# Three zero fills of a decode-attention backward kernel: two row blocks each of about 112 rows become one block of 208 to 223 rows

## The chip, the cores and the metric

The kernel runs on one core of a Trainium2 chip. The metric is the device time of one launch in microseconds (us), as the median of several runs.

## The reference, cut to what matters

The program computes a forward pass and all its gradients: attention of one query position over the last 4096 positions of a key and value cache, gated by a small two-layer network. What matters here is the size of two of the outputs, the gradients of the caches. Only the last W positions of 32768 take part, so the gradient of all the earlier ones is zero, and yet it has to be written.

```python
B, Hq, Hkv, Sk, Dh = 2, 32, 8, 32768, 128
W = min(4096, max(256, Sk // 4))              # 4096
k = jnp.repeat(k_cache[:, :, Sk - W:, :], rep, axis=1)
v = jnp.repeat(v_cache[:, :, Sk - W:, :], rep, axis=1)
scores = jnp.einsum("bhqd,bhkd->bhqk", q, k) * (Dh ** -0.5)
p = _softmax(scores, axis=-1)
o = jnp.einsum("bhqk,bhkd->bhqd", p, v)
...
s = attention(xn) @ wo
g = silu(relu(xn @ w1 + b1) ** 2 @ w2 + b2)
return x + s * g          # and its vjp with grad_out, for every input
```

Each cache gradient has 2 x 8 heads of 32768 rows of 256 bytes (128 bf16 values). Of every head 28672 rows (7168 KB) are zeros: 32 such blocks, 235 MB in all, of some 280 MB written.

## The kernel before, in words

**The zero fills.** There are 32 fills, numbered 0 to 31, one for each head of `out_2` (key gradient) and `out_3` (value gradient). They are copied by DMA from `zt`, an SBUF tile of 14336 zero bytes in each of 128 partitions. `zf` (L90) makes one DMA of a fill: `nent` entries (one row of the access pattern each) of `rows` consecutive cache rows, `rep` times over. The DMA casts while it copies. Up to 112 rows the zero bytes become bf16, two bytes out for one byte in. Above 112 rows the output is looked at as float32, four bytes out for one byte in, so that one entry can reach 224 rows, 57344 bytes:

```python
w = rows * DH
if w > ZG * DH:           # ZG = 112
    v = v.bitcast(F32)
    w //= 2
```

Fills 0 to 30 go out in order on POOL's (GpSimd's) DMA queue, L229 to L233. Those in `zlong` are one DMA of 128 entries of 224 rows. The eight in `zshort` are divided: a few small DMAs on a few entries, a main part of 128 entries, and a rest of single rows. In fills 2, 4, 6, 13 and 20 the main part is one DMA; in 8, 10 and 15 it is two, of 112 rows and of 96, 107 or 111 rows. POOL has eight DMA semaphores for these and waits with each issue for the DMA that is eight places ahead of it. The first fill waits for the load of `wo` (L235). Fill 31 goes out at the very end on SP's queue (`fin`, L640), in rows of 14336 bytes, after every other DMA that SP issues.

**The attention.** Four rounds, each for one batch entry and four key heads. Tiles `vnat` and `knat` hold the 4096 positions of a round's values and keys, in 128 partitions of 32768 bytes. Each has one buffer only, so a round goes so:

- `scores` (transposes at L383, matmuls at L390) over `vnat`, then over `knat`;
- the softmax and its gradient (L437 to L465);
- `outer_store` (its matmul is L417) for the values: the gradient is written over `vnat`, and stored on ACT's queue (L421); then SP loads the next round's values into the same tile (L210), as soon as that store has landed;
- the same for the keys: `contract` (its matmul is L406), `outer_store`, the store on ACT's queue, the next load on SP's queue.

So at the end of each round there is a chain: store, load into the same tile, and then the next round's `scores`.

**The end.** After the fourth round come the weights' gradients: `wq` is stored at L580 and `wo` at L586 (ACT's queue), `w2T` at L609, `dw` at L635 and fill 31 at L640 (SP's queue).

Of the kernel before, what the change touches and what calls it, by code (L numbers as in the profile page):

```python
# [16 lines left out]
def kernel(  # L17
# [72 lines left out]
    def zf(o, q, r0, nent, rows, rep=1):  # L90
# [18 lines left out]
        2: ((5, 8, 2), (120, 68, 3), (128, 32, 1), (16, 1, 1)),  # L109
        4: ((3, 1, 2), (2, 99, 6), (128, 214, 1), (86, 1, 1)),  # L110
        6: ((3, 1, 2), (3, 53, 2), (128, 221, 1), (60, 1, 1)),
        8: ((4, 82, 6), (128, 112, 1), (128, 96, 1), (80, 1, 1)),
        10: ((4, 69, 2), (128, 112, 1), (128, 107, 1), (88, 1, 1)),
        13: ((2, 20, 2), (3, 30, 2), (128, 221, 1), (124, 1, 1)),
        15: ((4, 1, 2), (128, 112, 1), (128, 111, 1), (120, 1, 1)),
        20: ((4, 25, 2), (128, 222, 1), (56, 1, 1)),
    }
    eps_t = const.tile([P, 1], F32, name="eps_t")
# [552 lines left out]
```

## Time and profile before

| | |
|---|---|
| median of 3 runs | 764.79 us (764.75 to 764.82) |
| profiled execution, its own time | 764.8 us |
| its span, first to last instruction | 763.0 us |
| bytes moved, mean rate | 326.73 MB, 428 GB/s |
| of these on POOL's queue (q0) | 227.55 MB in 6784 packets |
| on SP's queue (q1) / ACT's queue (q10) | 56.63 MB / 41.95 MB |
| busy: TensorE / VectorE / ScalarE | 52% / 36% / 28% |

A packet is the piece that a DMA engine moves at one go; the core has 16 DMA engines, and each queue has a share of the packets of every one of them. The profile gives for a stretch of time the number of packets of each queue, their bytes, and the time that they took as a share of the 16 engines. [...]

### The profile page before, as it was taken

To read this page: it belongs to the slowest core of one execution; us is meant where nothing else is said; L and a number is where in the kernel's file an instruction comes from. 1 tells how busy PE (TensorE), PEld (TensorE's weight loads), DVE (VectorE), ACT (ScalarE), POOL (GpSimd) and SP (SyncE) were. 2 spreads that over 40 slices of the span, in tenths; PEclk is the share of its full clock that TensorE was granted. 3 is DMA by queue.
4 is the path that set the end of the run, shared out by engine and by line. 5 is a ranking of instruction groups with operands and counts; after the bars stand their busy time and mean duration, and the time that the engine had idled before them with its cause. 6 is when DMAs were issued, how large, how long until landed. Compare 5 with 4: busy or idle time off the path is not lost.

```text
span 763.0 us, 9422 instructions
## 1 busy us (share of the span) xinstructions
PE 398.6 (52%) x4127; PEld 242.3 (32%) x4136; DVE 274.7 (36%) x481; ACT 216.7 (28%) x314; POOL 32.0 (4%) x63
## 2 busy tenths in 40 slices
PE   5866973853035748640187485002644784866900
PEld 4742552420023534210055341002433443323200
DVE  4334342823012455330054555001324451665600
ACT  3253323523001145430022455000114230721600
POOL 0200000000000100000000000000000000000000
PEclk9986896766558857665579577555767595855555
DMA  9999999999999999999999999999999999999998
GB/s 382 439 424 437 410 443 434 435 423 433 419 436 440 419 440 434 427 426 431 431 429 443 431 431 422 432 430 445 426 436 437 431 434 434 415 432 434 421 426 378
DMA packets 10973, 326.73 MB, mean 428 GB/s; under 512 B 2548, under 2 KB 2557, under 8 KB 2586
## 3 DMA queue, kind: packets, MB, share of 16 engines
q0 software_dynamic: 6784, 227.55, 70.4%
q1 hardware_dynamic: 2696, 56.63, 21.1%
q10 hardware_dynamic: 1452, 41.95, 15.2%
q8 instruction: 32, 0.52, 0.3%
q14 instruction: 9, 0.07, 0.0%
HBM read 45.62 MB, written 280.50 MB: 427 GB/s over the span
## 4 chain that ended last, share of the span: by engine, by line
PE 34%; DMA 33%; DVE 12%; ACT 10%; issue 7%; ACTq 0%; DVEq 0%; SPq 0%
DMA out_dram<-nat 16%; DMA nat<-in_A_k_cache_dram 10%; PE ov L417 7%; PE tp L383 6%; DMA nat<-in_A_v_cache_dram 5%; ACT tring L150 3%; ACT p_bf L451 2%; ACT nat L150 2%; DVE nat L152 2%; PE ps L406 2%; PE s_ps L390 2%; DVE ds_bf L464 2%; PE wps L584 2%; PE dops L331 1%; DVE tring L152 1%
## 5 line engine op out<-in xcount | busy, mean ns | idle before, releaser
L383 PE MATMUL tp<-pperm,nat 128*128 128x128 bf16 x1024 | 93.3, 244 | 178.0 <-DMA nat<-in_A_v_cache_dram 146.1
L152 DVE COPY tring<-tp 128x1024 bf16<-128x1024 bf16 (+1 forms) x98 | 66.3, 689 | 192.1 <-PE tp L383 188.7
L383 PEld LDWEIGHTS <-nat 128*128 128x128 bf16 x1024 | 69.4, 109 | 198.4 <-DMA nat<-in_A_v_cache_dram 148.1
L150 ACT CAST nat<-ov 128x512 bf16<-128x512 f32 x160 | 87.7, 590 | 78.5 <-PE ov L417 57.7
L150 ACT COPY tring<-tp 128x1024 bf16<-128x1024 bf16 (+1 forms) x34 | 34.4, 1011 | 247.6 <-PE tp L383 220.6
L152 DVE CAST nat<-ov 128x512 bf16<-128x512 f32 x96 | 65.7, 690 | 69.3 <-PE ov L417 66.9
L417 PE MATMUL ov<-bd,ds_bf 128*128 128x512 bf16 x124 | 50.0, 483 | 19.0 <-issue 12.9
L101 POOL DMA_DIRECT2D out_dram<-zt x54 | 30.4, 567 | 531.3 <-DMA out_dram<-zt 510.1
L417 PE MATMUL ov<-bd,p_bf 128*128 128x512 bf16 x123 | 46.7, 447 | 5.5 <-ACT nat L150 1.4
L406 PE MATMUL ps<-t,nat 128*128 128x16 bf16 x1024 | 28.8, 173 | 18.2 <-issue 11.4
L406 PEld LDWEIGHTS <-nat 128*128 128x128 bf16 x1024 | 28.7, 103 | 21.1 <-issue 16.0
L152 DVE CAST wq<-wps 128x512 bf16<-128x512 f32 x16 | 11.0, 690 | 54.4 <-PE wps L577 54.2
L390 PEld LDWEIGHTS <-zz 128*32 128x32 bf16 x512 | 17.6, 96 | 33.6 <-issue 23.5
L150 ACT CAST wq<-wps 128x512 bf16<-128x512 f32 x16 | 9.4, 586 | 63.6 <-PE wps L577 63.6
L390 PE MATMUL s_ps<-tring,zz 128*32 128x256 bf16 x256 | 20.0, 301 | 11.2 <-ACT tring L150 7.5
L398 PE MATMUL tp<-ident_bf,p_bf 128*128 128x128 bf16 x64 | 7.5, 310 | 34.9 <-ACT p_bf L451 34.9
L390 PE MATMUL dp_ps<-tring,zz 128*32 128x256 bf16 x256 | 20.0, 319 | 7.4 <-ACT tring L150 5.0
L451 ACT ACTIVATE p_bf<-e_sb,rl 32x512 bf16<-32x512 f32 x16 | 22.8, 1423 | 3.4 <-DVE rl L448 3.3
L417 PEld LDWEIGHTS <-ds_bf 128*128 128x128 bf16 x128 | 13.4, 111 | 27.4 <-issue 25.6
L464 DVE SCALAR_TENSOR_TENSOR ds_bf<-dp_ps,delta,p_bf 32x512 bf16<-32x512 f32 x16 | 21.6, 1352 | 0.2
L417 PEld LDWEIGHTS <-p_bf 128*128 128x128 bf16 x128 | 12.8, 109 | 19.7 <-issue 16.8
L398 PEld LDWEIGHTS <-p_bf 128*128 128x128 bf16 x64 | 6.5, 144 | 35.8 <-ACT p_bf L451 35.8
(198 smaller groups left out, 465.1 us busy)
## 6 DMA issues: line engine op xcount, KB each, us to landing
out_dram<-zt POOLq DMA_DIRECT2D x23, 7168.0 KB, 98.8
out_dram<-nat ACTq DMA_DIRECT2D x8, 4096.0 KB, 41.3
nat<-in_A_v_cache_dram SPq DMA_DIRECT2D x4, 4096.0 KB, 38.4
nat<-in_A_k_cache_dram SPq DMA_DIRECT2D x4, 4096.0 KB, 39.6
out_dram<-zt POOLq DMA_DIRECT2D x2, 7072.0 KB, 68.9
out_dram<-zt POOLq DMA_DIRECT2D x3, 3584.0 KB, 93.2
out_dram<-zt SPq DMA_DIRECT2D x1, 7168.0 KB, 35.0
out_dram<-zt POOLq DMA_DIRECT2D x1, 7104.0 KB, 120.6
```

The lines of the kernel that those rows point to most:

```text
L101: sw_fill.append(nc.gpsimd.dma_start(out=v, in_=zs))
L150: nc.scalar.copy(out=out_ap, in_=in_ap)
L152: nc.vector.tensor_copy(out=out_ap, in_=in_ap)
L331: nc.tensor.matmul(dops[0:B, :, :], lhsT=dsT_bf[:, dk, :], rhs=woT[:, :, dk, :], start=(dk == 0), stop=(dk == DK - 1))
L383: nc.tensor.transpose(tp[:, j, :], nat[:, g * CC + half * CH + j, :], pperm[:].rearrange("p b k -> p (b k)"))
L390: nc.tensor.matmul(out_ps[pr * RB:(pr + 1) * RB, half * CH * PB:(half + 1) * CH * PB], lhsT=zbuf[:, pr, o:o + RB], rhs=tT[:, :, pr, :], st ...
L398: nc.tensor.transpose(tp[:, cc, :], src[:, half * CH + cc].rearrange("r k b -> r (k b)"), ident_bf[:, :])
L406: nc.tensor.matmul(ps[:], lhsT=nat[:, g * CC + half * CH + cc, :], rhs=cols[half][:, cc, :, g, :], start=(half == 0 and g == 0 and cc == 0 ...
L417: nc.tensor.matmul(ov[:], lhsT=src[:, cc].rearrange("r k b -> r (k b)"), rhs=bd[:, gh * 4:(gh + 1) * 4, :], start=True, stop=True)
L451: nc.scalar.activation(out=p_bf[rb, :, :, pr], in_=e_sb[rb], func=ACT.Copy, scale=rl[rb, 0:1])
L464: nc.vector.scalar_tensor_tensor(out=ds_bf[rb, :, :, pr], in0=dp_c[rb], scalar=delta[rb, 0:1], in1=p_bf[rb, :, :, pr], op0=ALU.subtract, o ...
L584: nc.tensor.matmul(wps[:], lhsT=o_rows[:, j:N:NJ], rhs=ds_rows[:, :], start=True, stop=True)
```

## The change

The main part of fills 8, 10 and 15 becomes one DMA of 128 entries of 208, 219 or 223 rows (53248, 56064 and 57088 bytes an entry) and takes the float32 way of `zf`. The small parts ahead of it and the rest behind it stay as they are.

```diff
-        8: ((4, 82, 6), (128, 112, 1), (128, 96, 1), (80, 1, 1)),
-        10: ((4, 69, 2), (128, 112, 1), (128, 107, 1), (88, 1, 1)),
+        8: ((4, 82, 6), (128, 208, 1), (80, 1, 1)),
+        10: ((4, 69, 2), (128, 219, 1), (88, 1, 1)),
...
-        15: ((4, 1, 2), (128, 112, 1), (128, 111, 1), (120, 1, 1)),
+        15: ((4, 1, 2), (128, 223, 1), (120, 1, 1)),
```

## The prediction

> **What bounds the kernel now.** I read the page first, for how full the DMA engines are, then windows over single stages, then the timelines of SP and of TensorE for who waits where. The page's second part:
>
> ```profile
> DMA  9999999999999999999999999999999999999998
> GB/s 382 439 424 437 410 443 434 435 423 433 419 436 440 419 440 434 427 426 431 431 429 443 431 431 422 432 430 445 426 436 437 431 434 434 415 432 434 421 426 378
> ```
>
> The 16 DMA engines are full from the first slice to the last, while TensorE has half of its span. So the end is set by the bytes: 326.73 MB at 428 GB/s are 763 us. The fills (70% of the bytes) are filler that moves whenever nothing else does. The chain of compute costs time only where it leaves the DMA engines without work. That is the question for this change: it leaves the bytes written alone, but it alters **how long a load waits beside a fill**.
>
> The loads of the keys for rounds 2, 3 and 4, on SP's timeline, and what TensorE did about two of them, on its own timeline (in brackets the idle time ahead and what ended it):
>
> ```profile
> 217.44 0.54 SPq L210 DMA_DIRECT2D nat<-in_A_k_cache_dram  x1
> 375.28 0.54 SPq L210 DMA_DIRECT2D nat<-in_A_k_cache_dram  x1
> 516.33 0.54 SPq L210 DMA_DIRECT2D nat<-in_A_k_cache_dram  x1
> ```
>
> ```profile
> 250.74 1.89 PE L383 MATMUL tp<-pperm,nat 128*128 128x128 bf16 x16 [8.28 <-DMA nat<-in_A_k_cache_dram]
> 562.38 1.89 PE L383 MATMUL tp<-pperm,nat 128*128 128x128 bf16 x16 [12.40 <-DMA nat<-in_A_k_cache_dram]
> ```
>
> From issue to landing these three equal loads of 4096 KB took 33.3, 25.9 and 46.0 us (landed at 250.7, 401.2, 562.3). TensorE waited 8.3 us for the first and 12.4 us for the third. For the second it waited not at all, but without reserve: its timeline runs straight from the value transposes into the key transposes at about 401.4, 0.2 us after the landing. By the packet records, the first load ran beside fill 8, the second beside fill 15, both in halves of about 112 rows, and the third beside whole fills of 224 rows. (Fill 10's main part moved at about 257 to 280, when no load or store was under way, so its change costs nothing.)
>
> Why the third is slow can be read from the queues in two windows, 226:238 (first load, fill 8) and 530:548 (third load, whole fills):
>
> ```profile
> DMA packets 187, 5.21 MB, mean 435 GB/s; under 512 B 14, under 2 KB 14, under 8 KB 14
> ...
> q1 hardware_dynamic: 91, 2.92, 57.0%
> q0 software_dynamic: 95, 2.28, 44.8%
> ```
>
> ```profile
> DMA packets 192, 7.77 MB, mean 431 GB/s; under 512 B 15, under 2 KB 15, under 8 KB 15
> ...
> q0 software_dynamic: 95, 4.59, 59.3%
> q1 hardware_dynamic: 97, 3.18, 42.1%
> ```
>
> In both, fill packets and load packets go one for one (95 to 91, 95 to 97). The rate is the same, 435 and 431 GB/s, but the load's part of it is 2.92 of 5.21 MB against 3.18 of 7.77 MB.
>
> [...] here one row of 57344 bytes is one packet. [...] In the trace this is a packet of 4 bytes on each engine, and it is where the third load loses much. In the stretch 552.9:556 fourteen of them held 163% of the engines:
>
> ```profile
> q1 hardware_dynamic: 14, 0.00, 163.2%
> ```
>
> That is 1.632 x 16 x 3.1 / 14 = 5.8 us each, spent behind fill packets of over 2.1 us; 11 of that load's 16 took 6.4 us. Those of the first and second load took 0.03 us each, beside halves. [...]
>
> **The change part by part.**
>
> *Work of the DMA engines.* Per engine and fill, eight packets of 28 KB and eight of 24 to 28 KB become eight of 53 to 57 KB. In the packet records 28672 bytes take 1.079 us, 24576 take 0.928 and 57344 take 2.155. Two halves of fill 8 (2.007 us) against 53248 bytes at the long rows' rate (2.001 us): 0.006 us x 8 packets is 0.05 us. With three fills and three semaphore packets fewer, the gain is **0.2 us at most**. Half as many SBUF bytes are read, which buys nothing, since 28 KB and 56 KB rows already run at one rate. POOL issues 51 fill DMAs, not 54; at 0.57 us each that is 1.7 us of an engine with 32 us of work, hidden behind its waits. Its eight semaphores then reach further ahead in bytes, and since fills already wait 32 us or more from issue to landing, their queue is not empty either way.
>
> *Key load of round 2 (beside fill 8).* Now: a turn is 0.448 x 16 x 12 / 95 = 0.905 us for a fill packet and 0.570 x 192 / 91 = 1.20 for a load packet; eight turns (128 packets over 16 engines) are 16.9 us. After: from the other window 0.593 x 288 / 95 = 1.80 us for 48.3 KB, so 1.98 for 53248 bytes, and 1.25 for the load; eight turns are 25.9. The start, from issue to first packet, was 4.2, 6.7 and 10.3 us in the three loads; it is bounded by these, and I take 7. For the semaphore 0 to 10.6 us were seen, and I take the commonest beside long rows, 6.4. Sum 39.3, against 33.3 now: **+6.0 us**. It is not more, because the present landing is that of one straggling engine: its last packet began at 248.4, where seven eighths of all had begun by 237.7, since it was already in fill 9's long rows. Bounds: 0 (every engine just like the straggler) and +12.7 (like the third load, 46.0).
>
> *Key load of round 3 (beside fill 15).* No straggler here: 25.9 us. After: 7 + 8 x (2.12 + 1.25) + 6.4 = 40.4, so +14.5, less the 0.2 of reserve: **+14.3 us**. Bounds: 4.2 + 27.0 + 0 = 31.2, so +5, and 46.0, so +20.
>
> The loads and stores of round 4 already run beside long rows and stay as they are. Behind a late key load stands everything of the round: the key scores, the softmax, both stores on ACT's queue and the next two loads on SP's. So the sum carries to the last instruction: the compute is late by 6.0 + 14.3 = **20.3 us** (5 to 32.7).
>
> *What of it reaches the end.* Two more windows, after the issue of the `wo` store (712.5) and of the last DMA (727.1); the last two columns are the DMA share and GB/s:
>
> ```profile
> 712.50:727.10 14.60, 12.13 (x29) 3.29 (x27) 9.10 (x15) 8.44 (x15) 0.00 (x0) 0.50 0.99 421
> 727.10:763.00 35.90, 0.00 (x0) 0.00 (x0) 0.00 (x0) 0.00 (x0) 0.00 (x0) 0.50 0.93 400
> ```
>
> The last four DMAs (`wo` 4.19 MB, `w2T` and `dw` 1.84 each, fill 31 7.34) are 15.2 MB, and after 727.1 still 35.9 x 400 = 14.4 MB of them move. So of the 6.15 MB between 712.5 and 727.1 all but 0.8 are older: when `wo` is issued, the engines have 5.3 MB, 12.6 us at 421 GB/s, in hand. With the other queues slower the fills are faster, so this older work still ends at about 726. A `wo` store that comes later than that, less a start of some 1 us, finds idle engines. **The reserve is about 12 us** (10 to 14), and past it the end moves one for one: 20.3 - 12 = +8.3 us. With the 0.2 of gain this is +8 on the profiled execution's 764.8 us (span 763.0 and 1.8 around it), which is the median's 764.79 as well: **773 us**.
>
> **The rivals.** *The reserve swallows it* (not slower): the delay at `wo` stays under 12 us. The place is the gap between the older DMA work and the `wo` store, the price 20.3 us against 12, and it decides at 12. For it: the straggler, which may make round 2 cost nothing, and the semaphores, which are late beside long rows in some transfers only (the value load landing at 378.4 had nine of 16 on time); with both, 5 to 9 us. Then 764.6 us, the byte bound less 0.2. Against it: round 3's turns alone add 8.6 us, without any late semaphore. *Every wait at its worst*: 46 us for both loads and later stores that lose the help they now get from small packets (while a fill's single rows pass, each 256-byte packet costs a store one turn of some 0.03 us). Then 32.7 - 12 and more, 785 us. *Faster*: less for the engines to do is worth 0.2 us; beyond that only the uneven finish could give, and the last slice at 378 GB/s leaves about 2 us in it; 763 us at best. *That it doesn't do what it says*: rows of 57344 bytes already go as single packets, so rows of 53 to 57 KB will too.
>
> **How the numbers follow.** Two runs' medians can be told apart here from about 0.2%, 1.5 us, so slower begins at a delay of 13.5 us. Of my 5 to 32.7 us, most lies above: slower 0.72, of which 0.1 for the worst case; swallowed 0.22; faster 0.06. The range goes from the swallowed case, 764.2, to just short of the worst, 784.
>
> **What would show it.** Right: the key loads of rounds 2 and 3 take some 39 and 40 us, TensorE waits about 14 us for each, the last fill but one lands near 726 as now, and a gap in the DMA row stands ahead of the `wo` store, with all slices before it full. Wrong: the loads stay under 34 and 30 us, or the last instructions come 20 us later with no gap and no later end, or the rate in the middle falls under 425 GB/s.

## The result and the profile after

The changed kernel takes **786.6 us** (median of 6 runs, 782.59 to 799.47) against 764.88 us. It is slower, as forecast, but by 21.7 us and not by 8, and outside the range (764.2 to 784). The run at 799.47 us, more than 1.5% above the fastest of this kernel, is left out of the ratio of the two means, which is **1.0269** (95% interval 1.0246 to 1.0292). The profiled execution took 787.2 us with a span of 785.4, 22.4 us longer than before.

The page's second part, of the kernel after; compare the third number from the right of the GB/s row:

```profile
DMA  9999999999999999999999999999999999999099
GB/s 383 429 433 429 418 447 423 439 419 430 432 439 436 426 433 425 434 432 435 427 435 437 433 429 431 423 437 428 433 431 438 436 423 442 415 430 398 1 382 392
```

The same bytes (326.73 MB) move at the same rate (431 GB/s in the stretch 20:700 of both), except in one slice, in which nothing moves. In two windows, up to the `wo` store and from it on (columns as in the prediction: the last two are DMA share and GB/s):

```profile
726.50:748.00 21.50, 17.58 (x49) 8.08 (x50) 13.61 (x23) 7.67 (x14) 0.00 (x0) 0.50 0.00 1
748.00:785.40 37.40, 11.50 (x27) 3.09 (x25) 8.54 (x15) 8.13 (x14) 0.00 (x0) 0.50 0.96 407
```

The gap of 21.5 us is nearly the whole loss of 22.4. ACT issues the store at its end, first the line of the kernel before, then of the kernel after:

```profile
712.50 0.37 ACTq L586 DMA_DIRECT2D out_dram<-wo  x1
```

```profile
747.35 0.37 ACTq L586 DMA_DIRECT2D out_dram<-wo  x1
```

That is 34.9 us later than before; the store's first packet begins 0.9 us after its issue. The older DMA work was done at about 726.5, as forecast. The delay arises between two places in round 3, on SP's and TensorE's timelines. SP after, then TensorE before and after:

```profile
376.95 0.54 SPq L210 DMA_DIRECT2D nat<-in_A_k_cache_dram  x1
```

```profile
401.38 0.62 PE L383 MATMUL tp<-pperm,nat 128*128 128x128 bf16 x8
```

```profile
429.30 1.04 PE L383 MATMUL tp<-pperm,nat 128*128 128x128 bf16 x8 [21.09 <-DMA nat<-in_A_k_cache_dram]
```

The key load of round 3 is issued 1.7 us later than before and lands 28.0 us later, at 429.25 where it was 401.2: 52.3 us in place of 25.9. TensorE, which had not waited for it at all (the line of before has no wait), waits 21.1 us.

### The profile page after: what moved, and what is told of

Its sections match the earlier page's. It is cut to its first block, busy times and chain, and to the rows that moved or that the text cites. A ratio compares the mean times of both kernels' runs of the same rounds, so it can differ in the third digit from the quotient of the medians.

```text
span 785.4 us, 9428 instructions
## 1 busy us (share of the span) xinstructions
PE 396.8 (51%) x4136; PEld 240.0 (31%) x4136; DVE 274.9 (35%) x481; ACT 216.4 (28%) x314; POOL 30.3 (4%) x60
## 2 busy tenths in 40 slices
DMA packets 10541, 326.73 MB, mean 416 GB/s; under 512 B 2500, under 2 KB 2509, under 8 KB 2538
## 4 chain that ended last, share of the span: by engine, by line
PE 32%; DMA 31%; DVE 11%; ACT 9%; issue 7%; another core or an unknown queue 7%; SPq 0%; ACTq 0%; DVEq 0%
DMA out_dram<-nat 15%; DMA nat<-in_A_k_cache_dram 10%; PE tp L383 6%; PE ov L417 6%; DMA nat<-in_A_v_cache_dram 5%; ACT tring L150 3%; ACT p_bf L451 2%; PE s_ps L390 2%; ACT nat L150 2%; DVE ds_bf L464 2%; DVE nat L152 2%; PE wps L584 2%; PE ps L406 1%; PE wps L577 1%
## 5 line engine op out<-in xcount | busy, mean ns | idle before, releaser
L150 ACT COPY tring<-tp 128x1024 bf16<-128x1024 bf16 (+1 forms) x34 | 34.4, 1011 | 278.7 <-PE tp L383 253.8
L417 PE MATMUL ov<-bd,ds_bf 128*128 128x512 bf16 x128 | 50.5, 477 | 21.1 <-issue 15.9
L417 PE MATMUL ov<-bd,p_bf 128*128 128x512 bf16 x128 | 49.2, 457 | 4.0 <-DVE nat L152 1.4
L101 POOL DMA_DIRECT2D out_dram<-zt x51 | 28.7, 569 | 514.2 <-DMA out_dram<-zt 493.2
L406 PE MATMUL ps<-t,nat 128*128 128x16 bf16 x1024 | 28.9, 173 | 18.3 <-issue 11.4
L406 PEld LDWEIGHTS <-nat 128*128 128x128 bf16 x1024 | 28.8, 103 | 21.1 <-issue 16.0
L398 PE MATMUL tp<-ident_bf,p_bf 128*128 128x128 bf16 x64 | 7.6, 312 | 34.9 <-ACT p_bf L451 34.9
L464 DVE SCALAR_TENSOR_TENSOR ds_bf<-dp_ps,delta,p_bf 32x512 bf16<-32x512 f32 x16 | 21.7, 1359 | 0.2
L417 PEld LDWEIGHTS <-p_bf 128*128 128x128 bf16 x128 | 13.0, 110 | 19.6 <-issue 16.8
```

The lines of the kernel that those rows point to most:

```text
L101: sw_fill.append(nc.gpsimd.dma_start(out=v, in_=zs))
L150: nc.scalar.copy(out=out_ap, in_=in_ap)
L398: nc.tensor.transpose(tp[:, cc, :], src[:, half * CH + cc].rearrange("r k b -> r (k b)"), ident_bf[:, :])
L406: nc.tensor.matmul(ps[:], lhsT=nat[:, g * CC + half * CH + cc, :], rhs=cols[half][:, cc, :, g, :], start=(half == 0 and g == 0 and cc == 0 ...
L417: nc.tensor.matmul(ov[:], lhsT=src[:, cc].rearrange("r k b -> r (k b)"), rhs=bd[:, gh * 4:(gh + 1) * 4, :], start=True, stop=True)
L464: nc.vector.scalar_tensor_tensor(out=ds_bf[rb, :, :, pr], in0=dp_c[rb], scalar=delta[rb, 0:1], in1=p_bf[rb, :, :, pr], op0=ALU.subtract, o ...
```

## The experiments

The kernel before ran beside each of these, at 764.82 to 764.89 us; "wo" is the time at which the `wo` store is issued (712.5 before). Unless said otherwise, a time is the median.

### One fill at a time

`e1_only15`, `e2_only8` and `e3_only10` each take one line of the change:

```diff
-        15: ((4, 1, 2), (128, 112, 1), (128, 111, 1), (120, 1, 1)),
+        15: ((4, 1, 2), (128, 223, 1), (120, 1, 1)),       # e1; fills 8 and 10 likewise in e2, e3
```

Expected of fill 15 alone:

> Fill 15 alone in one block of 223 rows (fills 8 and 10 as before). Theory T: the loss is the key load of round 3, which meets long fill rows and a completion write queued behind them. Then nearly all of the loss is here: the key load of round 3 takes some 45 to 55 us (25.9 before), the wo store is issued some 30 to 36 us later, and the end is 18 to 24 us later, 782 to 788 us. Rival S (all three edits add up): about a third to a half, 770 to 778 us. Rival P (three DMAs fewer move POOL's eight places and the order in time): a third, about 772 us.

Measured: 786.2 us, ratio 1.0277 (1.0260 to 1.0294). Key load of round 3 53.8 us, wo at 746.25.

Expected of fill 8 alone:

> Fill 8 alone in one block of 208 rows. Theory T: the key load of round 2 lands within 3 us of before, because one engine was already in long rows there; the wo store is late by less than the reserve of 12 us; 764.6 to 765.5 us. My forecast's term: 6 us later at wo, and still no later end. Rival S: 770 to 778 us. Rival P: about 772 us.

Measured: 764.75 us, ratio 1.0002 (0.9993 to 1.0010). Key load of round 2 landed at 249.5 (250.7 before), wo at 712.85.

Expected of fill 10 alone:

> Fill 10 alone in one block of 219 rows. Theory T: nothing, its main part moves when no load or store is under way: 764.6 to 765.2 us. Rivals S and P: 770 us or more.

Measured: 764.92 us, ratio 1.0000 (0.9991 to 1.0009). Two of its 13 executions were long ones: the profiled one, 769.18 us with wo at 729.3, which comes in useful below, and one of 801.29 us without a profile.

So **fill 15 alone makes the loss**, and the edits do not add up.

### Number of DMAs, length of rows, or the cast

`e4_short51` has 51 fill DMAs like the changed kernel, but short rows:

```diff
+        8: ((4, 82, 6), (128, 104, 2), (80, 1, 1)),
+        10: ((4, 69, 2), (128, 109, 2), (108, 2, 1)),
+        15: ((4, 1, 2), (128, 111, 2), (124, 2, 1)),
```

> As few fill DMAs as in the changed kernel (51), but rows of 104 to 111: the main parts of fills 8, 10 and 15 are each one DMA of 128 entries, two rows blocks each (128,104,2), (128,109,2), (128,111,2), with the rest of fills 10 and 15 in entries of two rows. Theory T: the length of the rows decides, so this is as before: 764.5 to 766 us, key load of round 3 at 24 to 30 us. Rival P: as the changed kernel, 780 us or more.

Measured: 764.85 us, ratio 1.0000 (0.9991 to 1.0008); key load of round 3 26.9 us. The number of DMAs and POOL's semaphores have no part in it.

`e6_f32short` keeps the length of fill 15's two halves, and changes the cast alone:

```diff
-        if w > ZG * DH:
+        if w > ZG * DH or (o is out_2 and q == 15 and rows > 90):
```

> The kernel before, with fill 15's two halves (112 and 111 rows) written as float32 too: rows of 28 KB out of 7 KB of zeros. Same packets as before by length, but each is read from as few bytes a byte written as the long rows are. Theory L (the length of a packet written decides): as before, key load of round 3 at 24 to 30 us, 764.6 to 765.5 us. Rival C (the float32 cast decides, [...]): the load starts some 10 us late and its completion writes wait 5 us or more; key load at 38 us or more, and 770 us or more.

Measured: **784.26 us**, ratio 1.0251 (1.0223 to 1.0279). TensorE's timeline shows the landing of the changed kernel, to 0.1 us:

```profile
429.30 1.04 PE L383 MATMUL tp<-pperm,nat 128*128 128x128 bf16 x8 [27.57 <-DMA nat<-in_A_k_cache_dram]
```

So it is not the length of the row, as I had it, but **the float32 cast**, four bytes written for each byte read. The packet records show where it works first. The time from the issue of round 3's key load to its first packet is 6.7 us beside bf16 halves, 11.8 beside rows of 223 by the float32 cast, 12.0 beside halves by the float32 cast. In between, fills alone move: these are the only queue rows of the stretch 376.1:381.9 of the kernel before (SP's load has been issued at 375.28), and of the stretch 377.8:388 of the changed kernel (issued at 376.95):

```profile
q0 software_dynamic: 93, 2.32, 94.5%
```

```profile
DMA packets 88, 4.46 MB, mean 437 GB/s; under 512 B 10, under 2 KB 10, under 8 KB 10
...
q0 software_dynamic: 88, 4.46, 102.8%
```

(The share passes 100% because records overlap: those of the rows of 57088 bytes last 2.146 us and follow each other at 2.10.)

Two runs measured this by itself. `e11_plain15` copies without a cast, one byte for one; `e12_f32quarter` uses the float32 cast in rows of a quarter of the length:

```diff
+        15: ((4, 1, 2), (128, 55, 4), (126, 4, 1)),            # e11
+        zsrc = zt[:].bitcast(BF16) if rows == 55 else zt       # e11
+        15: ((4, 1, 2), (128, 56, 3), (128, 55, 1), (120, 1, 1)),   # e12
+        if w > ZG * DH or rows in (55, 56):                    # e12
```

> The kernel before, but fill 15's main part is copied without a cast: rows of 55 out of bf16 zeros, (128,55,4), as many bytes read as written, and the rest in (126,4,1). Theory R [...]: in round 3 the key load's first packet comes 12 us after its issue with the float32 cast, 6.7 with the bf16 cast, and here 3 to 5 us; key load at 20 to 26 us, 764.6 to 765.5 us. If the cast has no part in it: 6 to 7 us to the first packet.

Measured: first packet 3.9 us after the issue, key load **19.6 us**, landing at 395.0; 764.94 us, ratio 1.0000 (0.9991 to 1.0009).

> The kernel before, but fill 15's main part in rows of 56 and 55 written as float32: packets of 14 KB out of 3.5 KB of zeros. Theory R [...]: first packet of round 3's key load again 11 to 13 us after its issue, as with rows of 223 and of 112 by this cast; 780 us or more. Rival N [...]: 3 to 5 us, and 765 us.

Measured: first packet 11.9 us after the issue, in packets of 14 KB as in those of 57 KB (11.8). Rival N is out. The expected time came only in part: the 18 runs lie in two groups, six from 764.8 to 770.0 us (ratio 1.0022, 1.0009 to 1.0035) and twelve from 781 to 787. The profiled one is of the first (770.03 us), with a key load of 38.6 us; of the twelve there is no profile.

Bytes written for a byte read against the delay: 1: 3.9; 2: 6.7; 4: 11.4 to 12.0 us (the 11.4 is of `e13` below). These three points are close to a straight line, about 1.2 us and 2.7 more for each byte. What makes the delay is not shown: a packet record has a queue, a start, a duration and the bytes moved, and the reads of the zeros are in no trace.

Nor is it one fixed amount for every load. The delays above are of a load that is issued while fills alone move. The value load of round 4 is issued while the key gradient's store moves too, and beside rows of the same float32 cast it waited 7.1 us for its first packet in the kernel before and 6.75 in the changed one. In `e5` and `e10` below, where the value load of round 3 still had packets to move, the key load waited 10.3 and 9.1 us.

### One engine out of sixteen

The late start is 5 us of the 26 that are lost. The packet records name no engine; packets that follow one another without a gap are taken here for one engine's, which is an inference. In the changed kernel, seven eighths of the key load's packets had begun by 400.6, which is 5 us later than before (395.7): up to there the late start is all. But the last began at 412.7, on one engine, and that engine's completion (the packet of 4 bytes at the end of its part) began at 416.1 and took 12.7 us. In the stretch 404:416 of the changed kernel the load's queue still moved four packets of data and two completions:

```profile
q1 hardware_dynamic: 6, 0.13, 2.6%
```

In the packet records of `e1`, `e6`, `e10` and the changed kernel one engine starts the long rows of fill 16 at about 384.5, in those without a loss (the kernel before, `e4`, `e11`) at about 394.5. From then on the load packets of the changed kernel's early engine are some 3.4 us apart (but for one pair), the time of one long row and one load packet (2.13 and 1.25 us).

First idea: it is the one engine without a part in fill 15's 120 single rows, which take 0.03 us each and so let the load pass. `e5_spread15` (on the changed kernel) and `e10_only15spread` (on the kernel before) write 128 of them, meant as eight for every engine:

```diff
+        15: ((128, 223, 1), (128, 1, 1)),
```

> The changed kernel (fills 8, 10 and 15 in long rows), but the single rows of fill 15 go over all 16 engines: (128,223,1) and (128,1,1) in place of (4,1,2), (128,223,1) and (120,1,1). The 120 single rows lie on 15 engines only, and the sixteenth goes straight on to the long rows of fill 16. Theory E (one engine): the load of round 3 is late because of that sixteenth engine, which has no single rows to let it pass. Then the key load of round 3 takes 27 to 34 us (53 in the changed kernel), the wo store is issued at most 12 us later than before, and the end is at 764.5 to 766 us. Theory T as I had it (long rows delay the load on every engine): still 45 us or more, 780 us or more.

Measured: 765.0, 785.9, 801.95 and 802.91 us; the profiled one is the first, with a key load of 32.9 us and wo at 721.8. There the load was issued as early as 372.0, so that its first packet came at 382.3, as in the kernel before (382.0). Inconclusive: the longer runs have no profile.

> Fill 15 alone changed, as (128,223,1) and (128,1,1), so that its single rows lie on all 16 engines; fills 8 and 10 as before. Theory E: key load of round 3 at 28 to 36 us, 764.6 to 767 us, where fill 15 with 120 single rows had 53.8 us and 786. Otherwise 780 us or more.

Measured: 784.0 us, ratio 1.0255 (1.0235 to 1.0276), key load 52.0 us. **The idea is out**: the single rows are not the reason. In the packet records the engine in question has single rows in the changed kernel too: eight are written within 0.1 us at 384.3, ahead of any packet of the load, and its first long row of fill 16 follows at 384.4. The other 112 come between 393.3 and 404.5, among the load's packets.

Second idea: the engine is ahead of the others in the fills' queue, and while no load packet holds it up it gets into fill 16, whose long rows then alternate with the load's packets. `e9_after_short16` puts fill 16 into bf16 rows of 112 on the changed kernel, `e13_only15_short16` with fill 15 alone changed:

```diff
-    zlong = (0, 1, 3, 5, 7, 9, 11, 12, 14, 16, 17, ...
+    zlong = (0, 1, 3, 5, 7, 9, 11, 12, 14, 17, ...
```

> The changed kernel, with fill 16 in rows of 112 (bf16) in place of 224. Theory E (in round 3 one engine of 16 has none of fill 15's single rows, meets fill 16's long rows, and so gets the key load's last piece and its completion late): the load still starts 12 us after its issue, but its last completion comes by 408; 28 to 36 us in all, the wo store at most 12 us late, 764.6 to 767 us. If the delay is made in fill 15 itself on all engines: 45 us or more, 780 us or more.

Measured: 794.95 (profiled), 765.03, 798.16, 784.24 us. Inconclusive for round 3, since that execution was already 18 us late in round 2. There the key load took 47.4 us: 11.4 to its first packet, and eight completions of over 14 us. So fill 8's long rows did there what fill 15's do, though in the profiles of the changed kernel and of `e2` they did not.

> Fill 15 alone in one block of 223 rows, fills 8 and 10 as before, and fill 16 in rows of 112 by the bf16 cast. Theory F (one engine is ahead in the fills and, while the load is kept waiting, gets into fill 16's long rows; there it takes 3.4 us for each load packet, and its completion is late): the load still starts 11 to 13 us after its issue, but ends on all engines by 408; key load of round 3 at 28 to 34 us, wo store at most 12 us late, 764.6 to 767 us. If fill 16 has no part in it: 50 us and more, 782 us or more.

Measured: **764.88 us**, ratio 1.0005 (0.9996 to 1.0014). Key load 30.6 us, with its first packet still 11.4 us after the issue and every completion taking 0.03 us. The load's queue in the stretch 404:416, in which three completions are left and no data, and TensorE's timeline:

```profile
q1 hardware_dynamic: 3, 0.00, 0.0%
```

```profile
405.03 1.03 PE L383 MATMUL tp<-pperm,nat 128*128 128x128 bf16 x8 [4.24 <-DMA nat<-in_A_k_cache_dram]
```

Against the 429.3 of the changed kernel that is 24 us back, from a fill that the change does not touch. So the loss is made by fill 15's cast and fill 16's long rows together: the first makes the load late, and the second catch it on one engine. (In fill 16, length and cast changed at once; which of the two matters there is not shown.)

The other profiles fit this as a race. In seven (before, `e2`, `e4`, `e5`, `e7`, `e8`, `e11`) the first packet of round 3's key load began between 379.3 and 382.3, and the first long row of fill 16 at 394.3 to 394.7. In six (the changed kernel, `e1`, `e3`, `e6`, `e10`, `e12`) the load's first packet began between 384.6 and 389.3, and the first long row of fill 16 at 384.4 to 384.7. `e3` is among the six although its fill 15 is that of the kernel before: there the key load was issued 2.9 us later, at 378.2, and took 34.4 us. So a late issue lost the race there as the cast does, and the kernel before wins it by only some 2.5 us (an estimate from 382.0, its first load packet, and 384.5). What losing costs differs: in `e3` and `e12` the last completion took 0.01 us and the load took 34.4 and 38.6 us; in the other four it took 12.7 to 14.8 us and the load 51.9 to 53.8. What decides between these two is not shown.

### The reserve at the end

`e7_delay5` and `e8_delay13` touch no DMA. They delay the chain of compute in round 4:

```diff
         group_sum(lsum, lp, ALU.add, sel, ALU.mult)
+        if r == NR - 1:
+            for _ in range(5):                   # 13 in e8
+                nc.vector.memset(tring[:], 0.0)
```

> The kernel before, with five clearings of the tile tring on VectorE in round 4, between the softmax sums and their reciprocal: a pure delay of the chain of compute by about 9 us, with no DMA touched. Theory of the reserve (12 us at the wo store): the store is issued about 9 us later and the end does not move, 764.7 to 765.2 us. Rival (no reserve, each us late is a us lost): 773 to 774 us.

Measured: 764.93 us, ratio 1.0001 (0.9992 to 1.0009), wo at 717.0. That is 4.5 us later and not the 9 expected, so the reserve was tried here with half of the delay that was meant.

> As the one with five clearings, but thirteen: a delay of some 23 us. Theory of the reserve: the end is later by the delay less 12, about 11 us: 775 to 777 us, with idle DMA engines just ahead of the wo store. Rival (no reserve): 787 to 789 us. Rival (the end is bound by bytes whatever the chain does): 765 us.

Measured: 769.77 us, ratio 1.0064 (1.0049 to 1.0079). The clearings took 22.9 us, but the store was only 18.5 us late (4.4 us of the delay were taken up on the way, about as in `e7`; hence less than expected), and the span 6.0 us longer. The DMA engines have no work from 726.5 to 731.8. The issue of the store:

```profile
730.96 0.37 ACTq L589 DMA_DIRECT2D out_dram<-wo  x1
```

With the other profiles this makes a line. In all that are late the span ends 38.0 to 38.1 us after the issue at wo: 729.3 and 767.4 (`e3`'s long run), 730.2 and 768.2 (`e12`), 731.0 and 769.0 (`e8`), 744.1 and 782.2 (`e6`), 746.3 and 784.3 (`e1`), 747.35 and 785.4 (the changed kernel). In those with wo from 712 to 722 (before, `e2`, `e5`, `e7`, `e13`) it ends at 762.9 to 763.2. They meet at 763.0 - 38.05 = 724.95: **the reserve is 12.4 us**.

### No long rows in whole fills

`e14_allshort` writes the 23 whole fills in bf16 rows of 112 (`zlong = ()`):

> The kernel before with all 23 whole fills as one DMA each of (128,112,2), rows of 112 by the bf16 cast; the divided fills as before. If the end is set by the bytes and the float32 cast only makes loads wait: the key load of round 4 at 26 to 34 us (46.0 before), the wo store issued 15 us earlier or more, and the end where it was, 764.5 to 766.5 us. If long rows are worth something to the engines: 767 us or more. If the chain of compute still counts: 755 us or less.

Measured: 765.66 us, ratio 1.0011 (1.0004 to 1.0017). Key load of round 4 31.4 us (46.0 before), and the `wo` store 73 us earlier:

```profile
639.23 0.37 ACTq L586 DMA_DIRECT2D out_dram<-wo  x1
```

The chain of compute gains 73 us and the end gains nothing: the bytes set it (326.73 MB at 428 GB/s, as before). Long rows in the whole fills are worth about 0.1%.

## Why the prediction was right or wrong

**Right: what sets the end.** Bytes at one rate (431 GB/s before and after), a reserve of "about 12 us" at the `wo` store (12.4 measured), beyond it one for one, and a gap just ahead of that store. Given the true delay of 34.9 us this gives 22.4, which is what came.

**Right: the work of the DMA engines.** At most 0.2 us was to be gained, and `e2`, `e3` and `e4` move nothing. Fill 10 costs nothing, as said.

**Wrong: the key load of round 2**, +6.0 us. It took 34.7 us where it had taken 33.3, and landed 1.1 us earlier than before, being issued 2.5 us earlier. Something near the low bound, "every engine just like the straggler", was the case: seven eighths of the packets had begun 2.7 us later than before (240.4 against 237.7), and four completions took 7.9 to 9.9 us, but the straggler was still the last, with its last packet at 247.65 (248.35 before). Why the first packet came after 5.1 us and not after 11.8 was not tried. In the changed kernel the load is issued 4.2 us before the last packet of the value load begins; in `e9`, where it waited 11.4 us, only 0.5 us before. That is an argument from two profiles.

**Wrong, and the step that failed: the size of the key load of round 3.** The prediction said 7 + 27.0 + 6.4 = 40.4 us, with 46.0 as the worst; it is 52.3. The start is 11.8 and not 7. The last engine's turns, from the first packet of all to the end of its own last, 25.2, are near the 27.0, in part by chance: they are turns with rows of fill 16 and not of fill 15, and on that engine alone. From there to the landing 15.3 us pass and not 6.4. I had bounded both by the key load of round 4, the slowest of the three at hand, and it is no bound: it has 10.3 to the first packet, and most of its completions took 6.4 us where this one took 12.7. Longer ones were at hand: three completions of round 3's value load in the kernel before took 14.8 us each.

**Wrong: what makes it slow.** "Long fill rows" in turn with load packets on every engine. Seven eighths of the load's packets begin within 11.8 us of the first, where it was 13.7 before; the turns of 3.4 us hold for one engine. That is the straggler that I had seen in round 2; for round 3 I wrote "No straggler here", and did not ask whether a later start would make one. And in fill 15 the row's length is not the cause, but the cast that comes with it (`e6`). In the windows that I compared, both had changed together, and so I could not tell them apart.

**Left out: what the delay meets on its way.** I let 20.3 us pass unchanged through round 4. The value load of round 3 already landed 6.4 us late, behind completions of up to 8.5 us. The late stores of round 3 then met other fills: from its issue, the value store took 41.2 us and not 35.1, the key store 53.9 and not 44.8, and the key load 41.1 and not 46.0. From 28.0 us at the landing in round 3 the delay grew so to 38.4 at the issue of round 4's key load, and was 34.9 at the `wo` store. My worst case had some of this, with too little weight.

## What to carry to other kernels

Here filler traffic kept the DMA engines full. A chain 73 us faster earned nothing (`e14`) and one 4.5 us slower cost nothing (`e7`); past a reserve of 12.4 us each us late at `wo` was a us lost, 38.0 to 38.1 us from there to the end in six profiles. Find such a reserve as the work that is still queued when the last large store is issued, and price a change in latency against it. A filler DMA that writes four bytes for each byte read was the worst neighbour here for a load that something waits for: the key load of round 3 took 30.6 to 53.8 us beside fill 15 written so, 25.9 to 34.4 beside the bf16 cast (before, `e4`, `e3`) and 19.6 beside a plain copy (`e11`). So try a plain copy, or the smaller cast, where such loads are under way. A kernel can be close to such a loss without showing it, as the long run of `e3` suggests (769.18 us, where the median is 764.92). And before blaming a packet's length, ask what else differs between the two stretches compared.

## What was not expected of the hardware

A load issued while fills alone moved waited the longer, the more bytes the fill wrote for each byte that it read: 3.9, 6.7 and 11.4 to 12.0 us behind zeros written one, two and four for one, and with four for one nearly the same in packets of 14, 28 and 57 KB (11.9, 12.0, 11.4 to 11.8). Why is not shown. In the key load of round 3 the last completion of four bytes took 12.7 to 14.8 us beside rows of 57 KB (the changed kernel, `e1`, `e6`, `e10`), while most of the others took 0.03. In the kernel before and the changed one, completions beside such rows mostly took multiples of 2.1 us (2.16, 4.27, 6.38, 8.49, 10.6, 12.7, 14.8), about the time of one to seven rows (2.13 to 2.16 us each). A whole kernel took 765.66 us with its whole fills in rows of 28 KB (`e14`) and 764.89 with rows of 57 KB, the same to 0.1%.
